# Attention before a mixture of slots: v loaded in rows of two keys, and scores in that key order

## The chip, the cores and the metric

The kernel runs on one core of a Trainium2 chip. The metric is the device time of one execution in microseconds. It is measured outside the profiler in several runs, and once more under the profiler; the trace and all durations come from that one profiled execution.

## The reference, cut to what matters

Causal attention with 16 beacon keys in front, which every query sees, and then a soft mixture of experts over the 4608 rows that come out of it.

```python
B, H, S, Nb, D = 8, 8, 576, 16, 64
k_all = concat([beacon_k, k], axis=2); v_all = concat([beacon_v, v], axis=2)   # 592 keys
scores = q @ k_all.T / sqrt(D)            # key j (after the beacons) is masked for query i < j
a = exp(scores - max); a /= a.sum(-1) + 1e-9
attn = a @ v_all                          # (8, 8, 576, 64)
x = attn.transpose(0, 2, 1, 3).reshape(4608, 512)
logits = x @ phi                          # 32 slots = 8 experts of 4
d = softmax(logits, axis=0); c = softmax(logits, axis=1)
slot_input = d.T @ x                      # (32, 512)
slot_out[e] = relu(slot_input[e] @ w1[e]) @ w2[e]      # w1 512x1024, w2 1024x512
out = c @ slot_out                        # (4608, 512)
```

## The kernel before, in words

**The loop.** Attention runs over 32 pairs, `n` = 4 `b` + `g`: batch `b` and the two heads 2`g` and 2`g`+1, which lie on the lower and upper 64 partitions of `qT` and `kT`. The order of instructions on every engine is written out by hand (`manual_schedule`): each engine runs its own in the order of the program. Three pairs are in work at once: scores and exponentials of `n`, the product with v of `n`-1, the transposes of the result of `n`-2.

**Scores** (`scores`, L284 to L303). Keys stand on partitions, queries along the free dimension. The 592 keys are cut in chunks of 128, `c` = 0 to 4, the last of 80; chunk 0 starts with the beacons. The queries are cut in five blocks (`QLO`, `QW`) so that chunk `c` is diagonal in block `c`. The parts of the triangle are packed into four banks of up to 496 columns per head (`BANKS`, `BLK`). For each bank, PE makes 2 to 8 products (L292; 64 partitions of contraction, 128 keys out), ACT one exponential of both heads (L296) into `expT`, and POOL one `affine_select` (L302), which sets what is above the diagonal to 0. The score tile `sc` has two buffers, so bank 2 has to wait for the exponential of bank 0 and bank 3 for that of bank 1.

**Product with v** (`attend`, L307 to L318). For each query block `i` and chunk `c` up to `i`, `expT` is the stationary operand (128 keys x 128 queries) and `vh` (65 columns, the last of ones, which gives the row sums) streams: 15 products a head (L316). `normalize` on DVE (L326 to L329) divides. `x_transposes` (L338), `logits` (L349), `dispatch` (L376) and `combine_t` (L415) feed the second part, some of them once a batch.

**Loads.** SP issues q, k and v. q and k come in blocks of 16 rows of 64 floats per partition (`load_block`, L145, 4096 bytes in a row, five buffers) and tails of 4 rows, and are transposed on PE (L261, `trps`) and cast by DVE (L266, L272). v comes by chunk with one key on a partition (`load_v`, L186 to L196): each row of 64 floats, 256 bytes, is a run of its own; POOL casts it to f16 (`cast_v`, L199). In pair `n`, SP's order is the part of v of batch `b`+2 that belongs to `g`, then blocks of q and k (L463 to L467), so v stands in the same queue ahead of q and k.

**Weights.** w1 and w2 come in 32 pieces of 512 KB of f16, read as 1 MB of float32, issued by POOL (L232, L237) in the order of `wpieces` (L201), `pieces(n)` of them in pair `n` (L165 to L171), 26 by the end of the loop and 6 behind it (L498). Experts 0 to 5 have memory of their own; the last eight pieces go into buffers that q, k, v or `exps[0]` used before (`tails`, L205 to L218), the very last, of w2 of expert 7, into `exps[0]`.

**The end.** After the loop come `hidden` (L520), `hidden_t`, `slot_out` (L550, tile `so`), the products of the last expert (`fin`, L571), and the output products (L612, `fps`), copied out by ACT and DVE in turn (L592, L594) and stored by SP.

Of the kernel before, what the change touches and what calls it, by code (L numbers as in the profile page):

```python
# [9 lines left out]
FP = mybir.dt.float32  # L10
F16 = mybir.dt.float16
BF = mybir.dt.bfloat16
AL = mybir.AluOpType
# [6 lines left out]
QLO = [0, 112, 240, 368, 496]  # L20
QW = [112, 128, 128, 128, 80]
# [3 lines left out]
JB = [(0, 16), (16, 32), (32, 36)]  # L25

TP = 4
KW = [128, 128, 128, 128, 80]


BLK = {}
for _i in range(4):
    BLK[0, _i] = QLO[_i]
for _i in range(1, 4):
    BLK[1, _i] = 496 + QLO[_i] - 112
BLK[0, 4] = 880
BLK[3, 3] = 960
BLK[2, 2] = 1088
BLK[2, 3] = 1216
for _c in range(1, 5):  # L40
    BLK[_c, 4] = 1344 + 80 * (_c - 1)
EXPW = 1664
EXPPAD = 1712


BANKS = [
    (0, 496, [(0, 0, 496, 0)]),
    (496, 464, [(1, 112, 384, 0), (0, 496, 80, 384)]),
    (960, 384, [(3, 368, 128, 0), (2, 240, 256, 128)]),
    (1344, 320, [(c, 496, 80, 80 * (c - 1)) for c in range(1, 5)]),  # L50
]


# [1 line left out]
def kernel(  # L55
# [12 lines left out]
    nc = tc.nc  # L68
    P = 128
    B, H, S, D = q.shape  # L70
    Nb = beacon_k.shape[2]
    E, Dm, F = moe_w1.shape
    NSL = moe_phi.shape[1]
    SPE = NSL // E
    NDC = Dm // P
# [3 lines left out]
    NC5 = 5  # L79
    DD = D + 1  # L80
# [3 lines left out]
    const = ctx.enter_context(tc.tile_pool(name="const", bufs=1))  # L84
    idb = const.tile([P, P], BF, name="idb")
    make_identity(nc, idb)
    idh = const.tile([P, P], F16, name="idh")
    make_identity(nc, idh)
    onesh = const.tile([P, P], F16, name="onesh")
    nc.vector.memset(onesh[:, :], 1.0)  # L90

    sel4 = const.tile([P, 4, NSL], F16, name="sel4")
    for j in range(4):
        for g in range(4):
            nc.vector.tensor_copy(out=sel4[32 * j:32 * j + 32, g, :],
                                  in_=idh[32 * j:32 * j + 32, 32 * j:32 * j + 32])
# [14 lines left out]
    KS = S + Nb  # L111
# [6 lines left out]
        nc.gpsimd.memset(t[:, NG * KS:], 0.0)  # L118
    for t in exps:
        nc.gpsimd.memset(t[:, :, EXPW:EXPPAD], 1.0)  # L120
    for t in vhs:
        nc.gpsimd.memset(t[:, :, :, D:DD], 1.0)

    sohs = [const.tile([P, Dm // 2], F16, name=f"soh{i}") for i in range(2)]
    rd = const.tile([P, NSL], FP, name="rd")

    es = ExitStack()
# [37 lines left out]
    def pieces(n):  # L165

        if n < 20:
            return n % 2 if n > 4 else 0
        if n < 24:
            return 1  # L170
        return 2 if n < 28 else 2 - n % 2  # L171

    loads = [(b, w, k) for b in range(B) for (w, k) in BLOCKS]

# [8 lines left out]
            loads.pop(0)  # L183
            load_block((q, k)[w], w, b, kk)

    def load_v(b, chunks=range(NC5)):  # L186
        for c in chunks:
            if c == 0:
                vs[b] = stv.tile([P, NC5, H, D], FP, name="vstag", tag="v")
                nc.sync.dma_start(out=vs[b][0:Nb, 0, :, :],  # L190
                                  in_=beacon_v[b].rearrange("h n d -> n h d"))
            lo = max(0, c * P - Nb)
            hi = min(S, (c + 1) * P - Nb)
            p0 = lo + Nb - c * P
            nc.sync.dma_start(out=vs[b][p0:p0 + hi - lo, c, :, :],  # L195
                              in_=v[b, :, lo:hi, :].rearrange("h p d -> p h d"))  # L196

    def cast_v(b, c):
        nc.gpsimd.tensor_copy(out=vhs[b % 2][0:KW[c], c, :, 0:D], in_=vs[b][0:KW[c], c, :, :])  # L199

    wpieces = [(e, m, j) for m, es_ in ((0, range(4)), (1, range(4)), (0, range(4, E)), (1, range(4, E)))  # L201
               for e in es_ for j in range(2)]
    wat = {}

# [78 lines left out]

    def scores(n, bank):  # L284
        b, g = divmod(n, NG)
        base, w, mms = BANKS[bank]
        sc = ps_sc.tile([P, 2, 512], FP, name="sc", tag="sc")
        for (c, q0, qw, col) in mms:
            for hh in range(2):
                po = 64 * hh  # L290
                k0 = g * KS + c * P
                nc.tensor.matmul(sc[:, hh, col:col + qw], kTs[b % 2][po:po + D, k0:k0 + P],  # L292
                                 qTs[b % 2][po:po + D, g * S + q0:g * S + q0 + qw],
                                 start=True, stop=True)
        ex = exps[n % 2]
        nc.scalar.activation(ex[:, :, base:base + w], sc[:, :, 0:w], AF.Exp, scale=scale)  # L296
        at, pat, cnt, cbase = {0: (0, [[0, 2], [1, 112]], 112, Nb),
                               1: (496, [[0, 2], [1, 128]], 128, 0),
                               2: (960, [[0, 2], [0, 2], [1, 128]], 256, 0),
                               3: (1584, [[0, 2], [1, 80]], 80, 0)}[bank]  # L300
        ap = ex[:, :, at:at + cnt]
        nc.gpsimd.affine_select(out=ap, in_=ap, compare_op=AL.is_ge, fill=0.0,  # L302
                                base=cbase, pattern=pat, channel_multiplier=-1)  # L303

    xs, avs = {}, {}

    def attend(n, hh):  # L307
        b, g = divmod(n, NG)
        h = 2 * g + hh
        if hh == 0:  # L310
            avs[n] = ps_av.tile([P, 2, 512], FP, name="av", tag="av")
        av = avs[n][:, hh, 0:NC5 * DD].rearrange("p (i d) -> p i d", d=DD)
        for i in range(NC5):
            for c in range(i + 1):
                o = BLK[c, i]
                nc.tensor.matmul(av[:, i, :], exps[n % 2][0:KW[c], hh, o:o + P],  # L316
                                 vhs[b % 2][0:KW[c], c, h, :],
                                 start=(c == 0), stop=(c == i))  # L318

    def normalize(n):  # L320
        b, g = divmod(n, NG)
# [99 lines left out]
    with tc.manual_schedule(engines={ET.PE, ET.DVE, ET.Activation, ET.Pool, ET.SP}):  # L421
# [4 lines left out]
                          in_=beacon_k[1:B].rearrange("b h n d -> (h n) b d"))  # L426
        load_v(0)
        load_blocks(1)
        phif = work.tile([P, NDC, NSL], FP, name="phif", tag="phif", bufs=1)
        nc.sync.dma_start(out=phif[:, :, :], in_=moe_phi.rearrange("(c p) e -> p c e", p=P))  # L430
        for _ in transposes(0, BLOCKS):
            pass
        load_blocks(3)
# [1 line left out]
        load_blocks(1)  # L435
        for c in range(NC5):
            cast_v(0, c)
        nc.vector.tensor_copy(out=phih[:, :, :], in_=phif[:, :, :])
        for n in range(NPAIR + 3):
            b, g = divmod(n, NG)  # L440
            live = n < NPAIR
# [20 lines left out]
                pass  # L462
            if live:  # L463
                if b + 2 < B:
                    load_v(b + 2, ((0,), (1,), (2, 3), (4,))[g])
                if b + 1 < B:
                    load_blocks(sum(kk < 2 for _, kk in turns(b)[g]))  # L467
                scores(n, 3)
# [10 lines left out]
            if 1 <= n <= NPAIR:  # L479
                attend(n - 1, 1)  # L480
                normalize(n - 1)
            if n == NPAIR:
                keep_busy(9)
            if n == NPAIR + 1:
                keep_busy(4)
            if n == NPAIR - 3:
                post = stv.tile([P, NC5 * 2 * Dm], F16, name="post", tag="v")

                sizw = post[:, 0:NDC * 288].rearrange("p (t x) -> p t x", t=NDC)
                siz = [sizw[:, :, NSL * e:NSL * e + NSL] for e in range(E)]  # L490
                hTA = post[:, 1152:2176].rearrange("p (c s) -> p c s", c=NFC)
                hTB = post[:, 2176:2944].rearrange("p (c s) -> p c s", c=NFC)

                rep = post[:, 2944:3968].rearrange("p (c s) -> p c s", c=NFC)
                nc.vector.memset(post[:, 0:1152], 0.0)
            if n == NPAIR - 2:
                nc.vector.memset(post[:, 2944:3968], 0.0)
# [167 lines left out]
```

## Time and profile before

| | |
|---|---|
| median of 3 runs | 222.66 us (221.1 to 224.29) |
| the profiled execution: time | 221.0 us |
| its span, first to last instruction | 219.3 us |
| mean granted TensorE clock | 0.89 |
| exponentials (L296), pairs 0 to 31 | 13.6 to 162.1 us of the span |
| last piece of weights lands | 188.2 us |
| first output product (L612) | 190.1 us |

The page gives for every engine its busy time; PEld is the loading of stationary operands, which overlaps PE. A row of 40 digits cuts the span into equal slices, in tenths. A line of a group gives count, busy time, mean duration of one and the idle time before it with what ended it. "64*128 64x496" is a matmul on a tile of 64 rows (contraction) by 128 columns (outputs) of the array with a moving operand of 64 partitions and 496 columns. Matmuls are pipelined: how fast they go is read from the distance of their starts, not from their durations.

### The profile page before, as it was taken

The numbers are of one execution on the slowest core, as the hardware profiler recorded it, in microseconds if no ns is written. First come the engines' busy times: TensorE is split into PE (matmuls) and PEld (weight loads), VectorE is DVE, ScalarE is ACT, GpSimd is POOL, SyncE is SP. The second block draws the span as 40 slices with busy tenths as digits, with TensorE's granted clock in tenths as the row PEclk, the third lists the DMA queues.
The fourth block names the chain that finished last, engine by engine and source line by source line (L and its number), as shares of the span: only waits on it lengthen the run. The fifth ranks groups of instructions, "written<-read, shape, count | busy, mean of one in ns | idle before, by whom it ended". The sixth has DMA issues, their size and how long they took to land.

```text
span 219.3 us, 8117 instructions
## 1 busy us (share of the span) xinstructions
PE 162.6 (74%) x3521; PEld 119.4 (54%) x3521; DVE 127.1 (58%) x292; ACT 121.1 (55%) x156; POOL 102.2 (47%) x222
## 2 busy tenths in 40 slices
PE   1565998699969959997698858977859975797500
PEld 1433776477757647776476646765648642453200
DVE  5412699558856964886588757783574530167400
ACT  2274778468766856876567748768850201174400
POOL 3035566646666473757366755897872000000000
PEclk9999999969997996999699999999997999655555
DMA  6999999999999999999999999799999999189995
GB/s 187 326 204 350 240 259 237 283 276 296 274 255 282 248 252 290 243 264 300 266 236 271 278 270 211 138 198 198 211 211 216 216 211 208 22 329 384 389 395 227
DMA packets 55779, 55.63 MB, mean 254 GB/s; under 512 B 41792, under 2 KB 43840, under 8 KB 54848
## 3 DMA queue, kind: packets, MB, share of 16 engines
q1 hardware_dynamic: 49088, 38.35, 60.6%
q0 software_dynamic: 6656, 16.78, 40.6%
q8 instruction: 27, 0.44, 0.8%
q14 instruction: 8, 0.07, 0.1%
HBM read 62.46 MB, written 9.44 MB: 328 GB/s over the span
## 4 chain that ended last, share of the span: by engine, by line
PE 38%; DMA 23%; ACT 13%; issue 9%; SPq 6%; POOL 4%; DVE 1%; ACTq 0%; POOLq 0%
ACT expT L296 11%; PE sc L292 10%; PE av L316 10%; DMA expT<-in_moe_w_dram 9%; DMA qkstag<-in_q_dram 6%; DMA wts<-in_moe_w_dram 5%; PE trps L261 5%; PE fps L612 4%; SPq L195 4%; PE xtps L338 3%; POOL expT L302 3%; DMA qkstag<-in_k_dram 2%; PE sips L376 2%; PE lgps L349 2%; SPq L145 1%
## 5 line engine op out<-in xcount | busy, mean ns | idle before, releaser
L296 ACT ACTIVATE expT<-sc 128x992 f16<-128x992 f32 (+3 forms) x128 | 104.0, 864 | 43.8 <-PE sc L292 39.2
L302 POOL TENSOR_SCALAR_AFFINE_SELECT expT<-expT 128x224 f16<-128x224 f16 (+3 forms) x128 | 55.1, 437 | 50.6 <-ACT expT L296 47.8
L292 PE MATMUL sc<-qT,kT 64*128 64x80 bf16 (+4 forms) x576 | 46.4, 260 | 12.8 <-ACT expT L296 11.1
L316 PE MATMUL av<-vh,expT 128*128 128x65 f16 (+1 forms) x960 | 43.7, 200 | 2.4 <-DVE x L329 1.5
L316 PEld LDWEIGHTS <-expT 128*128 128x128 f16 (+1 forms) x960 | 36.0, 102 | 9.9 <-issue 8.5
L261 PE MATMUL trps<-idb,qkstag 128*64 128x64 bf16 x1024 | 26.6, 208 | 19.0 <-DMA qkstag<-in_q_dram 8.9
L261 PEld LDWEIGHTS <-qkstag 128*64 128x64 bf16 x1024 | 22.3, 121 | 26.8 <-issue 13.4
L292 PEld LDWEIGHTS <-kT 64*128 64x128 bf16 x576 | 20.6, 99 | 23.5 <-issue 15.8
L199 POOL CAST vh<-vstag 128x512 f16<-128x512 f32 (+1 forms) x40 | 24.5, 612 | 12.4 <-DMA vstag<-in_v_dram 12.3
L342 DVE COPY xT<-xtps 128x576 f16<-128x576 f16 x32 | 14.6, 457 | 24.6 <-PE xtps L338 24.1
L266 DVE CAST qT<-trps 128x512 bf16<-128x512 f32 (+1 forms) x38 | 22.9, 628 | 9.3 <-PE trps L261 8.6
L329 DVE TENSOR_TENSOR x<-av,r 128x640 f16<-128x640 f32 x32 | 26.4, 825 | 1.1
L272 DVE CAST kT<-trps 128x512 bf16<-128x512 f32 (+1 forms) x38 | 22.8, 628 | 7.2 <-PE trps L261 6.8
L338 PE MATMUL xtps<-idh,x 128*128 128x128 f16 (+2 forms) x160 | 14.8, 226 | 0.9 <-issue 0.6
L612 PE MATMUL fps<-soh,eT 32*128 32x256 f16 x64 | 12.0, 408 | 1.8 <-ACT w1h L592 1.3
L338 PEld LDWEIGHTS <-x 128*128 128x128 f16 (+2 forms) x160 | 9.7, 102 | 2.1 <-DVE x L329 0.3
L612 PEld LDWEIGHTS <-eT 32*128 32x128 f16 x64 | 6.5, 134 | 7.0 <-issue 4.4
L592 ACT COPY w1h<-fps 128x1024 f32<-128x1024 f32 (+1 forms) x7 | 6.6, 951 | 5.1 <-PE fps L612 5.1
L232 POOL DMA_DIRECT2D w1h<-in_moe_w_dram x12 | 8.9, 739 | 0.0
L594 DVE COPY w1h<-fps 128x1024 f32<-128x1024 f32 (+1 forms) x6 | 6.7, 1134 | 2.9 <-PE fps L612 2.9
L328 DVE RECIPROCAL r<-r 128x10 f32<-128x10 f32 x32 | 6.9, 216 | 1.1
L326 DVE TENSOR_SCALAR r<-av 128x10 f32<-128x10 f32 x32 | 5.4, 169 | 3.3 <-PE av L316 1.7
(85 smaller groups left out, 129.4 us busy)
## 6 DMA issues: line engine op xcount, KB each, us to landing
qkstag<-in_q_dram SPq DMA_DIRECT2D x16, 512.0 KB, 7.6
qkstag<-in_k_dram SPq DMA_DIRECT2D x16, 512.0 KB, 8.7
vstag<-in_v_dram SPq DMA_DIRECT2D x24, 256.0 KB, 7.4
w1h<-in_moe_w_dram POOLq DMA_DIRECT2D x12, 512.0 KB, 9.3
w2h<-in_moe_w_dram POOLq DMA_DIRECT2D x12, 512.0 KB, 8.7
out_dram<-w1h SPq DMA_DIRECT2D x5, 1024.0 KB, 6.5
wts<-in_moe_w_dram POOLq DMA_DIRECT2D x5, 512.0 KB, 12.5
out_dram<-w2h SPq DMA_DIRECT2D x2, 1024.0 KB, 7.2
```

What stands on the lines that cost most here:

```text
L199: nc.gpsimd.tensor_copy(out=vhs[b % 2][0:KW[c], c, :, 0:D], in_=vs[b][0:KW[c], c, :, :])
L261: nc.tensor.matmul(tp[D * hh:D * hh + D, j * w:(j + 1) * w], src.bitcast(BF)[:, 1::2], idb[:, :].rearrange("p (g x t) -> p x g t", x=2, t= ...
L266: copy(out=qTs[b % 2][:, :].rearrange("p (x j) -> p x j", j=JN)[:, :, j0:j1], in_=tp[:, 0:nj * w].rearrange("p (j x) -> p x j", j=nj))
L272: copy(out=dst[:, :, Nb:].rearrange("p g (t j) -> p g t j", j=JN)[:, :, :, j0:j1], in_=tp[:, 0:nj * w].rearrange("p (j g t) -> p g t j", j ...
L292: nc.tensor.matmul(sc[:, hh, col:col + qw], kTs[b % 2][po:po + D, k0:k0 + P], qTs[b % 2][po:po + D, g * S + q0:g * S + q0 + qw], start=Tru ...
L296: nc.scalar.activation(ex[:, :, base:base + w], sc[:, :, 0:w], AF.Exp, scale=scale)
L302: nc.gpsimd.affine_select(out=ap, in_=ap, compare_op=AL.is_ge, fill=0.0, base=cbase, pattern=pat, channel_multiplier=-1)
L316: nc.tensor.matmul(av[:, i, :], exps[n % 2][0:KW[c], hh, o:o + P], vhs[b % 2][0:KW[c], c, h, :], start=(c == 0), stop=(c == i))
L329: nc.vector.tensor_tensor(out=xs[b][:, :, 2 * g:2 * g + 2, :].rearrange("p i h d -> p h i d"), in0=av[:, :, :, 0:D], in1=r[:, :, :].unsque ...
L338: nc.tensor.transpose(tp[:, QLO[i]:QLO[i] + QW[i]], xs[b][0:QW[i], i, 2 * t:2 * t + 2, :].rearrange("p h d -> p (h d)"), idh[0:QW[i], 0:QW ...
L342: nc.vector.tensor_copy(out=xTs[0][:, t, 0:S], in_=tp[:, :])
L612: nc.tensor.matmul(fp_[:, j - j0, 256 * h:256 * h + 256], eT[32 * g:32 * g + 32, c0 + j:c0 + TP * P:TP], soh[32 * g:32 * g + 32, :], start ...
```

## The change

v is loaded in rows of two keys: partition `p` gets keys 2`p` and 2`p`+1, 512 bytes in one run. This holds for the first 512 of the 592 keys (`NPAIRED`); the last 80 stay one to a row. So v stands on partitions in the order of pairs, and the scores have to come in that order: a group of 128 keys is a set of 64 even ones (slot 0) and one of 64 odd ones (slot 1), each made by a product whose stationary operand takes every second column of `kT`. Groups 0 and 3 land on the lower 64 partitions, groups 1 and 2 on the upper, so that two groups share a column of scores. Where a block has two diagonals (group 0 below, group 2 above, block A), a product of the identity with a mask of 0 and -2^60 is made first and the scores are added to it; the other diagonals are selected by POOL as before, in five selects for four. The tail of 80 keys is block T. Block A holds two query blocks, one on its lower and one on its upper partitions: for the first, av contracts 64 partitions only; for the other, all 128 against a copy `vhu` of v whose lower half is zero, made once a batch (`copy_upper`, on DVE). A head's product with v takes 17 matmuls instead of 15. The weight pieces come in another order and two more of them before the loop's end. Some small tiles move (`phif` into `acc`, `sohs` into `post`).

```diff
+NPAIRED = 512
+BIG = -2.0 ** 60
+BANKS = [(0, 464), (464, 464), (928, 416), (1344, 336)]
+AVS = [
+    [("A", 0, 64, 0), ("A", 1, 64, 1)],
+    [("B", 0, 128, 0), ("B", 1, 128, 1)],
+    [("D", 0, 128, 0), ("D", 1, 128, 1), ("A", 0, 128, -1), ("A", 1, 128, -2)],
+    [("E", 0, 128, 0), ("E", 1, 128, 1), ("C", 0, 128, 2), ("C", 1, 128, 3)],
+    [("F", 0, 128, 0), ("F", 1, 128, 1), ("H", 0, 128, 2), ("H", 1, 128, 3), ("T", 0, 80, 4)],
+]
...
+    vhu = const.tile([P, 2, H, DD], F16, name="vhu")
+    nc.gpsimd.memset(vhu[0:64, :, :, :], 0.0)
...
         if n < 20:
-            return n % 2 if n > 4 else 0
-        if n < 24:
-            return 1
-        return 2 if n < 28 else 2 - n % 2
+            return n % 2 if n > 2 else 0
+        return (1, 2, 1, 2, 2, 2, 2, 1, 2, 1, 2, 1)[n - 20]
...
-    def load_v(b, chunks=range(NC5)):
...
+    def load_v(b, parts=range(4)):
+        for part in parts:
+            if part == 0:
+                vs[b] = stv.tile([P, NC5 * H * D], FP, name="vstag", tag="v")
+            two = vs[b][:, 0:2 * H * 2 * D].rearrange("p (m h x) -> p m h x", m=2, h=H)
+            if part == 0:
+                nc.sync.dma_start(out=two[0:Nb // 2, 0, :, :],
+                                  in_=beacon_v[b].rearrange("h (p j) d -> p h (j d)", j=2))
+                nc.sync.dma_start(
+                    out=two[Nb // 2:P, 0, :, :],
+                    in_=v[b, :, 0:240, :].rearrange("h (p j) d -> p h (j d)", j=2))
+            elif part < 3:
+                p0 = 64 * (2 - part)
+                nc.sync.dma_start(
+                    out=two[p0:p0 + 64, 1, :, :],
+                    in_=v[b, :, 128 * part + 112:128 * part + 240, :].rearrange(
+                        "h (p j) d -> p h (j d)", j=2))
+            else:
+                nc.sync.dma_start(
+                    out=vs[b][0:80, 4 * H * D:].rearrange("p (h d) -> p h d", h=H),
+                    in_=v[b, :, NPAIRED - Nb:S, :].rearrange("h p d -> p h d"))
...
+    def copy_upper(b):
+        nc.vector.tensor_copy(out=vhu[64:P, :, :, :], in_=vhs[b % 2][64:P, 2:4, :, :])
+    wpieces = [(e, m, j) for m, es_ in ((0, (0, 1, 2, 3)), (1, (0, 1, 2, 3)), (0, (4, 5)), (1, (4,)),
+                                        (0, (6, 7)), (1, (5, 6, 7)))
...
+        if bank < 2:
+            mms = [(0, 112, 464, 0), (1, 112, 464, 0)]
+        else:
+            mms = [(0, 0, 112, 0), (2, 240, 128, 0), (3, 368, 208, 128), (2, 368, 208, 128)]
+            for hh in range(2):
+                nc.tensor.matmul(sc[:, hh, 0:P], idb[:, :], masks[sl][:, :],
+                                 start=True, stop=False)
+        for (grp, q0, qw, col) in mms:
             for hh in range(2):
                 po = 64 * hh
+                p0 = 64 if grp in (1, 2) else 0
+                k0 = g * KS + P * grp + sl
+                nc.tensor.matmul(sc[p0:p0 + 64, hh, col:col + qw],
+                                 kTs[b % 2][po:po + D, k0:k0 + P - 1:2],
                                  qTs[b % 2][po:po + D, g * S + q0:g * S + q0 + qw],
+                                 start=(bank < 2 or col > 0), stop=True)
+        if bank == 2:
+            for hh in range(2):
+                po = 64 * hh
+                k0 = g * KS + NPAIRED
+                nc.tensor.matmul(sc[:, hh, 336:416], kTs[b % 2][po:po + D, k0:k0 + P],
+                                 qTs[b % 2][po:po + D, g * S + 496:(g + 1) * S],
+                                 start=True, stop=True)
...
+            for k_, (blk, sl, rows, c) in enumerate(AVS[i]):
+                o = BLK[blk, sl]
+                vc = vhs[b % 2][0:rows, c, h, :] if c >= 0 else vhu[:, -1 - c, h, :]
+                nc.tensor.matmul(av[:, i, :], exps[n % 2][0:rows, hh, o:o + P], vc,
+                                 start=(k_ == 0), stop=(k_ == len(AVS[i]) - 1))
...
                 if b + 2 < B:
-                    load_v(b + 2, ((0,), (1,), (2, 3), (4,))[g])
+                    load_v(b + 2, (g,))
...
+            if live and g == 0:
+                copy_upper(b)
```

## The prediction

> **What bounds the kernel now.** I read first the busy shares, the clock and the DMA row of the page, then the windows cut at the batches' first exponential (L296), then single matmuls in the timeline, then the waits and the end of the chain.
>
> ```profile
> PE 162.6 (74%) x3521; PEld 119.4 (54%) x3521; DVE 127.1 (58%) x292; ACT 121.1 (55%) x156; POOL 102.2 (47%) x222
> PEclk9999999969997996999699999999997999655555
> DMA  6999999999999999999999999799999999189995
> ```
>
> DMA looks full to 188 us, which makes it the suspect; no compute engine does. The windows show more (busy us of PE, PEld, DVE, ACT, POOL; clock; DMA):
>
> ```profile
> 71.07:90.98 19.91, 16.45 (x418) 12.70 (x414) 13.89 (x33) 13.35 (x17) 11.08 (x23) 0.91 1.10 254
> 147.65:162.08 14.43, 10.64 (x249) 8.26 (x245) 7.67 (x20) 12.72 (x17) 11.04 (x23) 1.00 1.11 205
> 162.08:188.24 26.16, 19.45 (x282) 12.66 (x279) 9.26 (x24) 2.08 (x5) 4.02 (x9) 0.93 1.02 202
> ```
>
> A batch of four pairs takes 19.9 us with PE busy for 16.5. One undisturbed pair, n=16, on PE:
>
> ```profile
> 90.50 0.38 PE L292 MATMUL sc<-qT,kT 64*128 64x496 bf16 x2
> 90.81 0.71 PE L261 MATMUL trps<-idb,qkstag 128*64 128x64 bf16 x32
> 91.45 0.37 PE L292 MATMUL sc<-qT,kT 64*128 64x384 bf16 x4
> 92.03 0.34 PE L292 MATMUL sc<-qT,kT 64*128 64x128 bf16 x4 [0.21 <-ACT expT L296]
> 92.31 0.63 PE L316 MATMUL av<-vh,expT 128*128 128x65 f16 x15
> 92.86 0.32 PE L261 MATMUL trps<-idb,qktail 128*64 128x64 bf16 x8
> 93.11 0.32 PE L292 MATMUL sc<-qT,kT 64*128 64x80 bf16 x8
> 93.36 0.43 PE L338 MATMUL xtps<-idh,x 112*128 112x112 f16 x5
> ```
>
> PE stands still only 0.21 us, for the first exponential to free a score buffer. The pair is a ring: exponential of bank 0 (0.95), then on PE bank 2, half of av, bank 3, xtps, the other half of av, next bank 0, next exponential. Everything added to PE between bank 2 and the next bank 0 lengthens the pair. By the starts of the first exponentials, an undisturbed batch is 4.16 + 3.73 + 4.0 + 4.35 = 16.2 us; batches took 17.6 to 19.9, so some 3 us of each are stalls:
>
> ```profile
> PE sc L292 <- ACT expT L296: 11.1, 27, 1.6
> PE trps L261 <- DMA qkstag<-in_q_dram: 8.9, 3, 4.5
> PE trps L261 <- issue: 8.1, 5, 2.7
> ```
>
> The loads stall the loop at two places after the start: 2.56 us in pair 1, 1.88 in pair 6. The "issue" stalls are something else. All stand at every 256th PE instruction, and each time a 16,384-byte packet of the page's queue q8 (instruction) began 2.3 to 2.9 us before PE went on (128.53 to 130.88; 79.32 to 82.19). Over 19 such boundaries from 38 to 147 us this cost 11.9 us, some booked under other names; the clock records add three stretches of 3.4 us at half clock behind the longest, some 1.3 us each, about 16 us together. The end:
>
> ```profile
> 156.55 12.03 DMA wts<-in_moe_w_dram
> 168.65 0.47 issue
> 169.14 19.11 DMA expT<-in_moe_w_dram
> 188.28 1.88 PE fin L571 x8
> ```
>
> From 138 us on a weight piece lands every 2.47 to 2.6 us; the last lands at 188.24 and `fin` waits for it. But PE was not far behind: the `so` products of the weights already there ended at 182.1. Carried on without DMA waits (4 at 0.2, `fin` 18 at 0.11, the copies of `so1` and `soh` 0.58 and 0.42), the first output product comes about 185.4, not 190.1. So **DMA sets the end by only 4.7 us; a loop that ends later than that is itself the bound.**
>
> **The change part by part.** *Changes of tile shape.* Between matmuls of one shape starts stand 29 ns apart (av). From av to scores the last av and the first score stand 126 to 129 apart; scores to av 201 where 256 columns stream in 107; trps to scores 128; xtps to etps 130 against 33. Each change costs 0.10 us, whichever pair of shapes. In the built order adjacent matmuls of unlike shape go from 221 to 392: the mask is a 128*128 product ahead of 64*64 scores, the tail block T is 64*128, and the 64-row blocks A make av start in 64*128. Of the 171 more, 32 (bank 1 to the mask) lie in the 0.21 us wait; 139 x 0.10 = **13.9 us**. [...]
>
> *Mask products.* 4 a pair, 128 in all, 128 columns each; 128-column xtps start 56 ns apart: **7.2 us**.
>
> *Scores.* Columns per head go from 496, 464, 384, 320 to 464, 464, 416, 336. A 64*64 group of four has no row. Now two heads' tiles start 3 ns apart and stream together (496 columns in 0.207 us), and two column halves of trps do too (a couple per 31 ns for 64 columns). Bounds: four together, banks 2 and 3 stream 752 columns for 704, 0.02 us a pair; two at a time, 0.47 more (second rival). I take four together, nearest to both rows, 0.6 us. Bank 0's exponential has 928 elements for 992, which take 942 ns for 997, and its stream is 13 ns shorter: 32 x 0.068 = -2.2. ACT in sum is unchanged (3328 to 3360 elements a pair).
>
> *av* has 34 products a pair for 30: 128 x 29 ns = **3.7 us**. Sum on the ring 13.9 + 7.2 + 0.6 - 2.2 + 3.7 = 23.2 us, 0.72 a pair; pair 0 is bound by ACT, which leaves **22.5**.
>
> *Selects* go from 380 + 407 + 637 + 326 = 1750 ns a pair to four of 407 at most and one of 326, 1954. POOL waits 47.8 us for exponentials; without that cover 32 x 0.2 = 6.5. The masks built at the start are POOL work ahead of the first v. *copy_upper*, 8 on DVE, 1040 elements: between a 576-element f16 copy (457 ns) and a 1024-element one (691). It runs behind `normalize`, where DVE delays a transpose buffer by 0.4 us at worst: 0 to 3 us, taken at 0 because DVE waits 24.1 us for xtps.
>
> *v loads.* SP issues 40 for 48. Packets: 37,888 of 256 bytes become 16,384 of 512 and 5,120 of 256. Median packets took 13 ns (128 bytes), 18 (256), 46 (1024), 84 (2048), 159 (4096), a straight line, so an estimated 27 to 28 for 512. (37,888 x 18 - 16,384 x 27.5 - 5,120 x 18) / 16 engines = 8.7 us of DMA time, 1.1 a batch. On the path are 1.1 us in pair 1 and, three batches of v being ahead of it, pair 6's wait with its half-clock stretch, 2.9: **-4.0**. The rest hides under PE; it would all count only if the loop kept its pace. Bounds 0 and -8.7. [...]
>
> *Instruction stalls.* PE gets 1,024 instructions more, four boundaries at some 0.6 us: +2.5. DMA has 1.1 us a batch less to do and 3 us more time, so packets should wait less. Bounds +4 (no relief) to -16 (all gone); I take **-2**, since these packets waited just as long from 147 to 168 us with weights alone in flight.
>
> *Weights.* 28 pieces for 26 are issued before the loop's end, in another order; nothing waits for a weight before 171 us. The four left need 4 x 2.47 us, the last issued about 7 us behind the loop's end (169.14 against 162.08) as now: landed some 15 us behind it, needed 22 behind. So the 4.7 us of waiting go: **-4.7**. If this cover fails, they stay.
>
> Sum: 22.5 - 4.0 - 2 = 16.5, loop's end 162.1 to 178.6; less 4.7, span 219.3 to **231.1**. With the 1.7 us around the span (221.0 against 219.3) 232.8. The runs' median, 222.66, lies 1.7 above the profiled run, so I give **233**.
>
> **Rivals.** *The loop keeps pace and DMA is the bound: faster.* For it: the DMA row, and all stalls of the loop come over DMA. The last landing then moves by 8.7, 188.2 to 179.5, but PE is ready no earlier than 185.4 if the loop stays, so 221.0 - 4.7 = 216; 212 if the loop shortens by 4 too. Against: the 0.21 us of slack. It decides if less than some 6 us of the 22.5 reach the ring (4.0 + 2 come back), as when shape changes overlap waits.
>
> *Stalls go, PE pays: no change.* All 16 us of instruction stalls vanish: 221.0 + 22.5 - 4 - 16 - 4.7 = 218.8; half of them, 227. For it: lighter DMA; against: the stalls under weights alone.
>
> *The 64*64 tiles don't run four together: much slower.* Bank 0 +0.19, banks 2 and 3 +0.14 each, 0.47 x 31 = 14.6 us: 248. For it: nothing in the trace runs four quarters; against: halves do, both ways. [...]
>
> *v is not in longer packets* is no rival: the built SP order has rows of 128 elements.
>
> **How the numbers follow.** Forecast (226 to 240) 0.55; stalls go (218.5 to 227) 0.20; not four together 0.13; faster 0.12. A measurement of this kernel tells about 2% from no change, 218.2 to 227.1: faster 0.12, same 0.20, slower 0.68. The range leaves a few per cent at the fast end and a little more at the slow end: 216 to 245; the forecast's own is 226 to 240.
>
> **What would show it.** Pair 16's ring should be near 4.9 us for 4.16, mask and 64*64 scores 0.10 us apart, quarters a few ns apart; PE busier, waits on bank 2 unchanged; v packets of 512 bytes at 27 to 30 ns; no wait for the last weight ahead of `fin`; first output product near 202 us. I am wrong if pairs stay near 4.2, if the last weight still ends the wait, or if the "issue" stalls at 256-instruction steps fall below 5 us.

## The result, and the profile after

The changed kernel took 256.9 us in the median of six runs (250.9 to 265.0), the kernel before 223.9 in six runs beside it (221.1 to 225.5). The ratio is 1.133, with a 95% interval of 1.114 to 1.152; it is taken from the two least disturbed runs of the changed kernel, 250.9 and 254.2, and so lies below the ratio of the medians. Slower was forecast, at 233 us and with 245 as the upper end: the sign came, the size did not. The profiled execution took 257.8 us with a span of 256.0.

From the page of the changed kernel, the span, the busy times and the rows of the clock and of DMA:

```profile
span 256.0 us, 9223 instructions
...
PE 198.8 (78%) x4033; PEld 138.1 (54%) x4033; DVE 132.6 (52%) x300; ACT 125.9 (49%) x156; POOL 110.4 (43%) x263
...
PEclk9999997696895599979799959999999979995555
DMA  7999999999999869979669999999999999029995
```

PE is busy 36 us longer, where the terms of the forecast's ring come to 23. The clock row has nine digits of 7 or less ahead of its closing stretch, for five before. The DMA row is nearly as full as it was, though 39,200 packets move instead of 55,779.

Windows of the changed kernel, cut at the first exponentials of the batches (length of the window, busy us of PE, PEld, DVE, ACT, POOL; clock; DMA share; GB/s):

```profile
66.83:94.34 27.51, 23.21 (x482) 16.38 (x478) 14.31 (x34) 13.76 (x17) 12.15 (x29) 0.75 0.93 200
94.34:117.49 23.15, 20.15 (x482) 14.55 (x478) 14.32 (x34) 13.73 (x17) 12.29 (x29) 0.93 0.97 211
185.54:202.70 17.16, 13.51 (x305) 9.67 (x301) 8.80 (x22) 13.66 (x17) 11.36 (x26) 1.00 1.09 192
202.70:227.00 24.30, 21.05 (x303) 14.09 (x300) 9.72 (x26) 2.48 (x6) 2.96 (x6) 0.93 0.61 117
```

A batch took 22 to 29 us where it took 17.6 to 19.9. The first row is at a clock of 0.75 and PE stood idle for 4.3 us of it; both losses lie beside the added instructions. The DMA share there is 0.93 at 200 GB/s, where the window shown of before had 1.10 at 254: the engines are almost as busy and deliver less. The last row, from the loop's end to the first output product, has a DMA share of 0.61 for 1.02: in that stretch DMA is no longer full.

One undisturbed pair on PE, n=12 (start, us, instructions and the wait ahead of them):

```profile
95.34 0.27 PE L334 MATMUL sc<-mask,idb 128*128 128x128 bf16 x2 [0.15 <-ACT expT L353]
95.54 0.34 PE L341 MATMUL sc<-qT,kT 64*64 64x112 bf16 x8
95.81 0.21 PE L349 MATMUL sc<-qT,kT 64*128 64x80 bf16 x2
95.85 0.46 PE L380 MATMUL av<-vh,expT 64*128 64x65 f16 x6
96.14 0.22 PE L380 MATMUL av<-vhu,expT 128*128 128x65 f16 x2
96.20 0.44 PE L380 MATMUL av<-vh,expT 128*128 128x65 f16 x9
96.57 0.32 PE L300 MATMUL trps<-idb,qktail 128*64 128x64 bf16 x8
96.82 0.28 PE L334 MATMUL sc<-mask,idb 128*128 128x128 bf16 x2
97.03 0.34 PE L341 MATMUL sc<-qT,kT 64*64 64x112 bf16 x8
97.31 0.43 PE L401 MATMUL xtps<-idh,x 112*128 112x112 f16 x5
```

Read by starts, bank 2 now takes 95.34 to 95.85, 0.51 us for 0.28 before, bank 3 0.49 for 0.25, half of av 0.72 for 0.55; the other half adds 0.17 too. That is 0.81 a pair, less some 0.06 by the shorter first exponential. The pair took 4.92 us for 4.16: the ring did what was forecast, step by step.

The waits of PE in the changed kernel (us in total, times, longest):

```profile
PE trps L300 <- DMA qkstag<-in_q_dram: 8.5, 2, 4.4
PE av L380 <- issue: 6.2, 5, 3.1
PE sc L334 <- ACT expT L353: 6.2, 17, 0.9
PE trps L300 <- issue: 4.7, 4, 3.2
PE sc L334 <- issue: 4.4, 2, 2.5
PE sc L341 <- issue: 4.0, 2, 2.8
```

The waits named "issue" sum to 19.3 us in these rows; all such rows of before come to 10.3. The long ones fall on whatever instruction stands at a 256th place. The wait for q was 4.4 at the start and 4.05 in pair 1, where it had been 2.56; the one in pair 6 is gone, as forecast.

The end of the chain of waits:

```profile
218.23 1.91 PE so L617 x32
221.44 2.78 PE so L617 x24
224.23 0.98 PE fin L638 x8
227.75 1.03 PE fps L679 x8
```

`fin` follows `so` with no DMA ahead of it. The loop ends at 202.7 and the first output product comes at 226.3, 23.6 later; forecast was 23.3 from a chain without waits for weights. So 24.1 of the 24.9 us by which the forecast missed the span, 256.0 against 231.1, lie in the loop: it was to end at 178.6.

### The profile page after: what moved, and what is told of

It reads as the page before. It is cut to its first block, busy times and chain, and to the rows that moved or that the text cites. A ratio compares the mean times of both kernels' runs of the same rounds, so it can differ in the third digit from the quotient of the medians.

```text
span 256.0 us, 9223 instructions
## 1 busy us (share of the span) xinstructions
PE 198.8 (78%) x4033; PEld 138.1 (54%) x4033; DVE 132.6 (52%) x300; ACT 125.9 (49%) x156; POOL 110.4 (43%) x263
## 2 busy tenths in 40 slices
DMA packets 39200, 55.71 MB, mean 218 GB/s; under 512 B 8824, under 2 KB 27256, under 8 KB 38264
## 4 chain that ended last, share of the span: by engine, by line
PE 66%; ACT 9%; issue 9%; SPq 4%; DMA 4%; DVE 2%; POOL 0%; ACTq 0%
PE av L380 19%; PE sc L341 14%; ACT expT L353 8%; PE trps L300 6%; PE sc L334 6%; PE xtps L401 5%; PE fps L679 4%; DMA qkstag<-in_q_dram 4%; PE lgps L412 2%; PE so L617 2%; PE sc L349 2%; PE sips L439 2%; SPq L219 2%; PE hps L587 1%; PE etps L478 1%
## 5 line engine op out<-in xcount | busy, mean ns | idle before, releaser
L353 ACT ACTIVATE expT<-sc 128x928 f16<-128x928 f32 (+2 forms) x128 | 108.8, 870 | 80.6 <-PE sc L341 73.2
L380 PE MATMUL av<-vh,expT 128*128 128x65 f16 (+2 forms) x960 | 57.7, 205 | 6.3 <-issue 4.8
L341 PE MATMUL sc<-qT,kT 64*64 64x464 bf16 (+3 forms) x768 | 53.0, 324 | 4.9 <-issue 4.0
L380 PEld LDWEIGHTS <-expT 128*128 128x128 f16 (+2 forms) x1088 | 45.9, 104 | 15.4 <-issue 9.3
L357 POOL TENSOR_SCALAR_AFFINE_SELECT expT<-expT 128x256 f16<-128x256 f16 x64 | 26.9, 422 | 42.7 <-ACT expT L353 42.6
L361 POOL TENSOR_SCALAR_AFFINE_SELECT expT<-expT 64x256 f16<-64x256 f16 x64 | 25.6, 400 | 31.9 <-ACT expT L353 29.6
L300 PEld LDWEIGHTS <-qkstag 128*64 128x64 bf16 x1024 | 24.1, 129 | 23.8 <-issue 13.3
L334 PE MATMUL sc<-mask,idb 128*128 128x128 bf16 x128 | 19.6, 238 | 11.2 <-ACT expT L353 6.2
L341 PEld LDWEIGHTS <-kT 64*64 64x64 bf16 x768 | 17.5, 112 | 15.4 <-issue 6.1
L234 POOL CAST vh<-vstag 128x512 f16<-128x512 f32 x32 | 19.4, 609 | 13.8 <-DMA vstag<-in_v_dram 13.8
L380 PE MATMUL av<-vhu,expT 128*128 128x65 f16 x128 | 15.8, 206 | 1.4 <-issue 1.4
L389 DVE TENSOR_SCALAR r<-av 128x10 f32<-128x10 f32 x32 | 5.4, 169 | 17.6 <-PE av L380 17.5
## 6 DMA issues: line engine op xcount, KB each, us to landing
qkstag<-in_k_dram SPq DMA_DIRECT2D x16, 512.0 KB, 15.1
vstag<-in_v_dram SPq DMA_DIRECT2D x16, 256.0 KB, 10.7
```

The source lines that it names most:

```text
L300: nc.tensor.matmul(tp[D * hh:D * hh + D, j * w:(j + 1) * w], src.bitcast(BF)[:, 1::2], idb[:, :].rearrange("p (g x t) -> p x g t", x=2, t= ...
L334: nc.tensor.matmul(sc[:, hh, 0:P], idb[:, :], masks[sl][:, :], start=True, stop=False)
L341: nc.tensor.matmul(sc[p0:p0 + 64, hh, col:col + qw], kTs[b % 2][po:po + D, k0:k0 + P - 1:2], qTs[b % 2][po:po + D, g * S + q0:g * S + q0 + ...
L380: nc.tensor.matmul(av[:, i, :], exps[n % 2][0:rows, hh, o:o + P], vc, start=(k_ == 0), stop=(k_ == len(AVS[i]) - 1))
```

## The experiments

Two measures go through all of them, besides the time. *Stalls at 256 steps*: at every 256th of PE's instructions (matmuls and weight loads) from 20 us to the loop's end, the distance from the start of the one before it, as far as it is over 0.35 us; the table has the sum. *Half-clock windows* are stretches of 3.41 us that begin in the loop and have a granted clock of 0.5. A packet's time is the mean over all v packets of 512 bytes. Medians are of four runs, of six for the first two kernels; the other columns come from one profiled execution each.

*Wide* loads write all 128 partitions in one transfer; two kernels cut these transfers in two, by partitions or by heads. "v of two batches" loads v for the first two batches only and uses those values again. Where a kernel has one part of the change alone, v meets other keys than it should, and only its times are read.

| kernel | us (range) | 512-byte packet, ns | stalls, us | half-clock windows | loop's end |
|---|---|---|---|---|---|
| before | 223.9 (221.1 to 225.5) | 21 (256 bytes) | 10.2 | 4 | 162.1 |
| changed | 256.9 (250.9 to 265.0) | 46.3 | 17.6 | 12 | 202.7 |
| before, changed loads | 234.7 (232.4 to 242.6) | 43.9 | 21.7 | 9 | 177.1 |
| changed, loads of before | 245.2 (241.1 to 245.8) | 21 (256 bytes) | 5.8 | 7 | 185.8 |
| before, wide loads | 219.8 (217.9 to 222.4) | 29.8 | 12.6 | 4 | 161.6 |
| changed, wide loads | 238.2 (237.4 to 239.5) | 29.5 | 8.9 | 6 | 183.7 |
| before, wide in partition halves | 233.9 (231.2 to 235.3) | 42.4 | 19.6 | 9 | 176.3 |
| before, wide in halves by heads | 214.4 (212.8 to 216.8) | 29.9 | 9.6 | 2 | 157.5 |
| before, v of two batches | 206.6 (206.2 to 208.5) | none | 2.6 | 1 | 150.8 |
| changed, v of two batches | 232.5 (228.3 to 234.3) | 53.5 | 6.3 | 2 | 178.7 |
| changed wide, no mask products | 231.2 (229.5 to 236.8) | 29.8 | 7.4 | 6 | 175.0 |
| changed wide, fewer shapes | 230.0 (225.4 to 232.3) | 29.7 | 11.5 | 6 | 179.4 |
| changed wide, both | 227.9 (223.5 to 231.0) | 29.9 | 13.3 | 9 | 175.8 |
| changed wide, both, weights as before | 226.8 (224.9 to 231.4) | 29.9 | 15.1 | 4 | 171.1 |
| before, weights as changed | 227.7 (225.0 to 229.3) | 21 (256 bytes) | 10.3 | 7 | 173.5 |
| changed, weights as before | 254.7 (250.5 to 256.7) | 45.9 | 14.0 | 12 | 198.6 |

### Which part is it: the loads alone, the PE part alone

The kernel before with the changed kernel's `load_v` and `cast_v`:

```diff
-    def load_v(b, chunks=range(NC5)):
...
+    def load_v(b, parts=range(4)):
...
-                    load_v(b + 2, ((0,), (1,), (2, 3), (4,))[g])
+                    load_v(b + 2, (g,))
```

> The kernel before with the changed v loads alone (rows of 512 bytes onto 8, 120, 64 and 64 partitions, the casts that fit them); scores, products with v, weight order as before, so v meets the wrong keys and only the time counts. Theory 1 (the slow v loads cost time through queues: pair 1 waits longer, PE waits longer for its instructions): 512-byte packets 45 to 50 ns as in the changed kernel, undisturbed pairs still 4.16 us, stalls at 256-instruction steps 15 us or more for 11.9, time 228 to 236. Rival (the loads are harmless, the extra stalls come from PE's own extra instructions): 222 to 226, stalls near 12 us.

The ratio to before was 1.047 (1.036 to 1.059), +11.5 us by the medians (234.7 against 223.2 beside it), as the first theory expected. Undisturbed pairs stayed at 4.15 and 3.72: the loss is in stalls, 21.7 us for 10.2, and in five more half-clock windows. The wait for q in pair 1 hardly grew, 2.74 for 2.56. Longer packets, which were forecast to give time back, cost it.

The changed kernel with the load and cast of before:

```diff
-    def load_v(b, parts=range(4)):
...
+    def load_v(b, chunks=range(NC5)):
...
```

> The changed kernel with v loaded as before (rows of 256 bytes, one key to a partition, casts as before); all else as changed, so v meets the wrong keys and only the time counts. Theory 1: 256-byte packets near 20 ns, pair 1's wait back to 2.6 us, stalls at 256-instruction steps 12 to 15 us, undisturbed pairs still 4.9 us; time 232 to 240, which is what the prediction gave for the ring alone. Rival (PE's instructions make the stalls): 246 to 252.

245.2, +22.1 us, between the 232 to 240 expected and the rival's 246 to 252; undisturbed pairs 4.92, 4.60, 4.71, 4.82. The two parts sum to 33.6 us and the whole change measured 33.0 by the medians: within the spread of the runs, they add. PE's program is that of the changed kernel, and the stalls are the fewest of all kernels with full v traffic, 5.8 us. So the 1,024 added instructions do not make the stalls.

### Why the longer packets are slow

The changed loads write 8, 120, 64, 64 and 80 partitions at a time. These two runs put the same bytes into transfers over all 128 partitions (only the last 80 rows of 256 bytes are not), first in the kernel before, then in the changed kernel; the diff is against the changed loads:

```diff
-                p0 = 64 * (2 - part)
...
-                    out=two[p0:p0 + 64, 1, :, :],
...
+                    out=two[:, part, :, :],
+                    in_=v[b, :, 256 * part:256 * part + 256, :]...
```

> The kernel before with v in rows of 512 bytes too, but two transfers onto all 128 partitions (keys 0 to 255 and 256 to 511), then 64 and 16 rows of 256 bytes; the rest as before, v meets the wrong keys and only the time counts. Theory 1 (the 512-byte packets were slow because half of the partitions, or 120 by 15 engines, were written at a time): packets 27 to 30 ns, pair 1's wait near 1.5 us, time 214 to 221. Rival 2 (512-byte rows are slow wherever they land, for instance for the order in which they are read): packets 45 ns or more and the time of the run with the changed loads.

> The changed kernel with v in rows of 512 bytes on all 128 partitions as in the second run; all else as changed, v meets the wrong keys and only the time counts. Theory 1 (half-width transfers): packets 27 to 30 ns, pair 1's wait near 1.5 us, time 230 to 237, a little below the third run. Rival 2 (512-byte rows slow in themselves): no change, 248 to 256.

In the kernel before the ratio was 0.981 (0.971 to 0.992), in the changed one 1.065 (1.055 to 1.076) for its 1.133. The second time, 238.2, lies 1.2 us above what was expected. Packets took 29.8 and 29.5 ns for 43.9 and 46.3. By medians, which the forecast went by, that is 27 ns for 42 and 45: its 27.5 ns was right for a transfer over all partitions.

Wide differs from the change in more than partitions (order, number of transfers, the part of 120), so two controls in the kernel before cut each wide transfer in two. One cuts by partitions, the other by heads; transfers, packets and bytes are the same in both.

```diff
+                for r0 in (0, 64):
...
+                        out=two[r0:r0 + 64, part, :, :],
```

> The kernel before with the full-width v loads (219.8 us, 512-byte packets 29.8 ns) cut into two transfers each, partitions 0 to 63 and 64 to 127, 16 transfers of v more in SP's queue and nothing else. The packets and their number are the same. If the number of partitions that one transfer writes sets the packet's time: 43 to 47 ns, and a time near the first experiment's 234.7, between 230 and 237. Rival, the two halves run side by side and the first experiment was slow for another reason (its 120-partition part, its order): packets under 33 ns and 218 to 223.

```diff
+                for h0 in (0, 4):
...
+                        out=two[:, part, h0:h0 + 4, :],
+                        in_=v[b, h0:h0 + 4, 256 * part:256 * part + 256, :]...
```

> The control for the halves: the kernel before with the same full-width 512-byte loads, each cut into two transfers again, now by heads (0 to 3, 4 to 7), so that each still writes all 128 partitions. Transfers, packets and bytes are those of the run with halves. If the number of partitions decides: packets of 29 to 31 ns and 218 to 222 us. Rival, twice as many transfers of half the size are what costs: 42 ns and 231 to 236.

By partitions: ratio 1.058 (1.035 to 1.082). By heads: 0.969 (0.956 to 0.982), below the 218 to 222 us expected. The v transfers of the two runs, with the median us from issue to landing at the end of the line, and the queue that carries them (packets, MB, share of 16 engines); by partitions first, then by heads:

```profile
vstag<-in_v_dram SPq DMA_DIRECT2D x32, 256.0 KB, 9.0
q1 hardware_dynamic: 32704, 38.35, 59.7%
```

```profile
vstag<-in_v_dram SPq DMA_DIRECT2D x32, 256.0 KB, 7.2
q1 hardware_dynamic: 32704, 38.35, 56.0%
```

With the same counts and sizes, a v packet takes 42.4 ns in one and 29.9 in the other, and the kernels lie 19.5 us apart (the kernel before took 223.4 and 223.1 beside them). The partitions that a transfer writes make that difference. If all 16 engines are at work, 16 x 512 bytes in 42.4 ns are an estimated 193 GB/s, and 275 in 29.8. Why a transfer onto half of the partitions is slower, no run here shows. The rows of 256 bytes before, at 21 ns, are an estimated 195 GB/s over all partitions: the change exchanged one limit, which by this estimate was the length of the packets, for another of the same height.

Half of the partitions is not the whole story of the changed loads. In the last three batches of the changed kernel the transfer onto 120 partitions runs apart from the next one, and its packets (with the 64 onto 8 partitions ahead of it) took 37 to 40 ns on average, where those of the wide load at that place took 28 to 30. Why 120 partitions are slow as well stays open; how many engines carry that transfer no run shows. By heads is also 5 us quicker than the uncut wide load; why is open too.

### Do the stalls come from the load on DMA?

Both kernels with v loaded for the first two batches only:

```diff
-                if b + 2 < B:
-                    load_v(b + 2, ...)
+                if b + 2 < B and g == 0:
+                    vs[b + 2] = vs[b]
```

> The kernel before, which loads v for the first two batches only and uses those values again. If the stalls at every 256th PE instruction come from the load on DMA: they fall from 10 us to under 5, half-clock stretches in the loop nearly vanish, undisturbed pairs stay at 4.15 and 3.7 to 4.35, the loop ends at 148 to 153, the time is 201 to 210. Rival, the stalls are a fixed price of so many instructions: they stay at 9 to 11 us, and only the two waits for q go: 214 to 218.

> The changed kernel with v loaded for the first two batches only. With the load gone the ring alone is left: 12.7 us of start, 8 batches of 19.05 us and 3 to 5 us in the first batch end the loop at 168 to 172; with 23.5 to the first output product and 30 behind it 220 to 230 us. That minus the kernel before without v's loads is the PE part free of DMA: 18 to 23 us. Rival, the changed kernel's losses don't come from v's loads: 240 or more, with 15 us or more of stalls.

Before: 206.6, ratio 0.941 (0.923 to 0.959), stalls 2.6 us and one half-clock window, undisturbed pairs unchanged. PE's instructions are the same 3521, so the stalls were not a fixed price of so many instructions; they come with v's loads. PE's busy tenths and clock on the page of that run show a loop almost wholly at full clock:

```profile
PE   1463996798999999998999989958668976797300
PEclk9999999999999999999999999988999999855555
```

The changed kernel: 232.5, above the 220 to 230 expected, and 25.9 above the kernel before without these loads, for 18 to 23. From the second batch on it is the ring alone. A batch of it (columns as in the windows above):

```profile
60.36:79.50 19.14, 18.51 (x484) 13.73 (x484) 14.26 (x34) 13.78 (x18) 12.63 (x30) 1.00 0.71 180
```

PE is busy for 18.5 of 19.1 us: free of DMA's delays the changed kernel is bound by PE. The seven later batches take 137.0 us against 117.5 in the kernel before, 2.8 a batch, 0.70 a pair (forecast 0.72). The excess lies in the first batch, 28.4 us for 18.8, while v of two batches still comes in the narrow way, at 53.5 ns a packet, and a stall of 3 us stands at 38 us.

### The terms of the ring

On the changed kernel with wide loads (238.2 us), so that v's packets do not disturb. Without the mask products:

```diff
-                nc.tensor.matmul(sc[:, hh, 0:P], idb[:, :], masks[sl][:, :],
-                                 start=True, stop=False)
```

> The changed kernel with full-width v loads (238.2 us) without the 128 mask products; the second diagonal of the two shared blocks stays unmasked, and the order of v's rows is that of the wide load, so the values are others. By the ring: 128 x 56 ns = 7.2 us of products less, and 80 changes of tile shape less, of which 30 lie in the wait ahead of bank 2, so 50 x 0.10 = 5.0: 238.2 - 12.2 = 226, between 224 and 229; an undisturbed pair goes from 4.9 to 4.5. Rival, the products hide in waits that the ring has anyway: 236 to 239, pair 4.9.

231.2 (ratio to before 1.042, 1.031 to 1.054), 2 us above the 224 to 229 expected. Undisturbed pairs went from 4.92, 4.60 and 4.71 to 4.50, 4.30 and 4.40: 0.34 a pair, 11 us over 32, for 12.2 forecast. Of these, 7.0 reached the time.

The same work in fewer shapes:

```diff
-                nc.tensor.matmul(sc[:, hh, 336:416], kTs...[po:po + D, k0:k0 + P], ...)
+                for p0 in (0, 64):
+                    nc.tensor.matmul(sc[p0:p0 + 64, hh, 336:416], kTs...[po:po + D, k0 + p0:k0 + p0 + 64], ...)
...
-    [("A", 0, 64, 0), ("A", 1, 64, 1)],
+    [("A", 0, 128, 0), ("A", 1, 128, 1)],
```

> The changed kernel with full-width v loads (238.2 us), with the same work in fewer tile shapes: the tail's scores as two 64*64 halves, and the first query tile's av products contracted over 128 rows for 64, which mixes the other group's values in. Columns streamed on the path stay the same. 97 changes of shape less: 97 x 0.10 = 9.7 us, so 228.5, between 226 and 231, and an undisturbed pair at 4.6 for 4.9. Rival, the 0.10 us is only the tail of a stream that is paid whatever the shape of the next: 236 to 239.

230.0, inside the forecast; pairs 4.72, 4.29, 4.39 and 4.52, 0.28 less a pair, 9.0 us over 32 for 9.7. PE has 64 products more here and is quicker. Its trace has 302 changes of shape for 392, 90 fewer where 97 were counted ahead: 9.0 us for 90 of them is the 0.10 us that was taken.

Both at once:

> Both edits at once, no mask products and fewer shapes, on the changed kernel with full-width loads. If the terms of the ring add: 238.2 - 12.2 - 9.7 = 216, between 214 and 220, pair 4.2 to 4.3, which is about the kernel before with the same loads (219.8). If they overlap (one wait hides both): 222 to 226.

227.9: neither 214 to 220 nor fully the other case. The terms did add in the pairs, 4.30, 4.09 and 4.12, 0.57 less a pair or 18 us; only 10.3 came out in the time. Against the changed kernel with wide loads, stalls rose from 8.9 to 13.3 us and half-clock windows from 6 to 9. The weights' order was a suspect, and the next group takes it out.

### The weights' order

The kernel before with the changed order and spacing of the weight pieces:

```diff
-            return n % 2 if n > 4 else 0
+            return n % 2 if n > 2 else 0
...
+        return (1, 2, 1, 2, 2, 2, 2, 1, 2, 1, 2, 1)[n - 20]
...
-    wpieces = [(e, m, j) for m, es_ in ((0, range(4)), (1, range(4)), (0, range(4, E)), (1, range(4, E)))
+    wpieces = [(e, m, j) for m, es_ in ((0, (0, 1, 2, 3)), (1, (0, 1, 2, 3)), (0, (4, 5)), (1, (4,)),
+                                        (0, (6, 7)), (1, (5, 6, 7)))
```

> The kernel before with only the changed kernel's order and spacing of the weight pieces. My theory: DMA is full from 138 us on, so the last piece lands when it did (about 188 us): within 2 us of 223, and fin still waits for it. Rival, the earlier issue of two pieces brings the last landing forward by up to 4.9 us: 218 to 220, and no DMA wait ahead of fin.

Ratio 1.025 (1.011 to 1.039): neither theory. No DMA wait stands ahead of `fin`, as the rival had it, but the loop grew. The waits of that kernel, and the instruction where the longest stands:

```profile
PE trps L260 <- DMA qkstag<-in_q_dram: 18.8, 5, 6.7
```

```profile
148.97 1.06 PE L260 MATMUL trps<-idb,qkstag 128*64 128x64 bf16 x32 [6.70 <-DMA qkstag<-in_q_dram]
```

Pair 26 takes 11.7 us for 4.0. DMA is full in that wait (a share of 1.09 from 142 to 146 us), and the last batch's v and q share it with weight pieces issued earlier than before; that these pieces are what delays q is argued, not shown. A wait for weights at the end was exchanged for one for q in the loop, and a dearer one.

The old order and spacing put back into the changed kernel (the lines of `wpieces` are those above, the other way round):

```diff
...
-        return (1, 2, 1, 2, 2, 2, 2, 1, 2, 1, 2, 1)[n - 20]
+        if n < 24:
+            return 1
+        return 2 if n < 28 else 2 - n % 2
...
```

> The changed kernel with only the weights' order and spacing of before put back. In the kernel before the new order cost 4 us, through one wait for q in pair 26. If it costs the changed kernel the same: 251 to 254. If the longer pairs cover it (the trace of the changed kernel has no wait for q after 100 us): 254 to 260, with the weights' waits ahead of fin back by at most 2 us. I expect the second.

254.7, 2 us below the changed kernel and well inside its runs: no effect of the order shows there. There is no wait for a weight ahead of `fin` with the old order either: the loop ends at 198.6 us, and the first output product comes 24.0 us behind it.

And put back into the run with both ring terms out:

> No mask products, fewer shapes and full-width loads (227.9 us, where the ring's terms asked for 216), with the weights' order of before put back as well. If the order is what held that run back: 222 to 225. If it is not, and the shorter ring meets more stalls and half-clock windows whatever the order: 226 to 230.

226.8 for 227.9. There are fewer half-clock windows (4 for 9) but more stalls (15.1 for 13.3): the order was not what held that run back. Its undisturbed pairs are still 0.1 to 0.4 us longer than those of before, and it meets more stalls than the kernel before with the same loads. Why a ring almost as short meets more of them is open.

## Why the prediction was right in sign and wrong in size

**The ring** was right: 0.72 us a pair forecast, 0.76 in the undisturbed pair and 0.70 over seven batches without v's traffic. The two runs that took terms out came within 1.2 us of them: 11 for 12.2 with the mask products and the shape changes they bring, 9.0 for 9.7 with other shape changes; av had no run of its own. The rival in which the four tiles don't run together did not come: in the changed kernel's undisturbed pairs the 112-column and 128-column scores start 6 to 7 ns apart.

**The v loads, "-4.0", are the step that failed.** It took 27.5 ns for a 512-byte packet from a straight line through packets of other sizes; they took 46.3 (median 45). With all partitions written the line holds (29.5 to 29.9, median 27). What it left out was in the diff: `two[p0:p0 + 64, 1, :, :]`, transfers that write a part of the partitions. Its bounds, 0 and -8.7, left no room for loads slower than before. By the sum of packet times, v's loads and the other rows of 256 bytes took 56.4 us of the 16 engines for 50.4, where 8.7 less was forecast. The wait for q in pair 1 was to lose 1.1 us of its 2.56 and came to 4.05.

**"Instruction stalls, -2"** was argued from this relief of DMA and fell with it, in sign: 17.6 us for 10.2. Its two other reasons did not hold either: the added instructions bring no stalls (5.8 us with the loads of before), and with most of v's loads gone only 2.6 us are left, though weights, q and k still come. The two steps were forecast at -6 together and measured +11.5 in the run of the loads alone: 17.5 of the 23.9 us between 233 and 256.9. With loads over all partitions the same -6 would have been near (-3.4 uncut, -8.8 by heads).

**The PE part** was forecast at +17.8 (22.5 less 4.7) and measured +22.1 by the medians: another 4.3. The profiled execution, the quickest of its four runs, lies 20.1 above the profiled one of before (241.1 for 221.0), so 2 to 4 us are left, not clear of the spread of these runs. It has three half-clock windows more than before although its stalls are fewer, and in it av waited 1.6 us for one `copy_upper`, which took 2.57 us; how much these make was not separated. Of the rest, 1.2 us are the median of before, 223.9 beside these runs for the 222.66 used, and 1.5 a slip in the forecast: its sum, 232.8, starts from the profiled execution, and of the 1.7 us by which the median lay above that, 233 has only 0.2.

**Half-clock windows** were priced for the four there were, three at 1.3 us each inside the stalls' term and one inside the loads', and no step asked what makes them. They went from 4 to 12 (below).

**The tail, "-4.7"**, was right: from the loop's end to the first output product went from 28.0 us to 23.6, and the last weight landed 15.0 us behind the loop's end, as forecast. The terms of its chain come to 185.9 and not 185.4, which makes it -4.2. At a loop's end as late as 198.6 us the old order of the pieces does as well; at 177.1, near the forecast's 178.6, it does not: the kernel before with the changed loads still waits 1.6 and 1.1 us for weights ahead of and within `fin`, and its first output product comes 25.8 us behind the loop. Moving the pieces is not free either, as the kernel before with the new order shows.

**At nothing** were taken `copy_upper` and the selects. `copy_upper` took 0.43 us in the median of its 8 times, 0.81 at most, and in the changed kernel nobody waited for it; for the selects ACT waited 4.6 us, for 3.5 before.

None of the rivals had the loads slower than before. "The loads cost more" would have been the rival to price, with the rate of a load by the partitions it writes as its condition.

## What to carry to other kernels

A packet's length is one part of a transfer's price: packets of 512 bytes took 29.9 ns where each transfer wrote 128 partitions, 42.4 where it wrote 64. Count also the partitions that each transfer writes, and cut a transfer along another axis than partitions if it must be cut (214.4 us by heads, 233.9 by partitions). Where several waits and a bound engine share a loop, a term that is right on an undisturbed pair comes back only in part (10.3 of 18 us with both terms out): stalls and the clock take their share of it. Keep tiles of one shape together on PE: 90 changes of shape cost 8 us of the time here.

## What the runs showed of the hardware that I had not expected

**Windows at half clock followed windows in which PE was little busy.** The half-clock stretches begin on a grid of 3.41 us: in the kernel before at 44.75, 65.23, 82.30 and 106.19 us, 6, 5 and 7 steps apart. Windows of the kernel before cut on that grid (columns as above, the clock third from the end):

```profile
41.38:44.79 3.41, 1.83 (x60) 1.53 (x62) 1.61 (x3) 1.51 (x3) 1.76 (x4) 0.99 1.00 324
44.79:48.21 3.42, 3.42 (x76) 2.79 (x76) 1.48 (x4) 1.84 (x4) 1.82 (x4) 0.51 1.19 250
```

and of the changed kernel:

```profile
55.80:59.20 3.40, 0.28 (x9) 0.15 (x6) 0.09 (x1) 0.00 (x0) 0.59 (x2) 1.00 1.16 225
59.20:62.60 3.40, 3.40 (x59) 1.92 (x60) 2.92 (x8) 1.87 (x2) 0.96 (x2) 0.50 1.09 260
```

PE was busy for 1.83 of 3.41 us, and the next window ran at 0.51. Over the 14 kernels above with v's full traffic, of the full-clock windows that begin between 32 and 175 us with PE's matmuls busy for less than 55%, 44 of 45 were followed by a half-clock one (the other was busy for 54.9%); between 55 and 70%, 22 of 55; above 70%, none of 394. What decides in the middle group is open. So by these counts a stall of 1.5 to 3 us is paid twice when it falls into one window; a half-clock window of 3.41 us costs at most its half, an estimated 1.7 us. Ahead of the half-clock window at 65.2 us of the kernel before, one gap of 1.6 us was enough: PE was busy for 1.85 of the 3.41 us.

**PE's stalls at 256 steps grew and shrank with v's loads.** At the 18 stalls of over 0.7 us, before and changed, PE went on 2.2 to 3.1 us after a packet of 16,384 bytes of queue q8 (instruction) had begun, which itself took 0.9 to 1.5 us. That distance varies little while the stalls do, 0.7 to 3.4 us: by this the length of a stall goes with when the packet begins. That PE waits for its instructions out of this packet is read from these distances and from the queue's name. With PE's program of before, the stalls followed v's loads: 21.7 us with packets at 43.9 ns, 10.2 in the kernel before, 2.6 with most of v's loads gone. The time of v's packets is not all of it: the two kernels without mask products and with fewer shapes had 13.3 and 15.1 us at 29.9 ns.
